# A streaming x + alpha·fx on one core: the first store on the ACT queue, beside an fx load, both in rows of 4096 bytes

## The chip, the cores and the metric

The kernel runs on one core of a Trainium2 chip. The metric is the device time of one execution in microseconds (us); lower is better. Each time is one execution; the time before is the median of three.

## What is computed

```
B, S, D = 512, 32, 640          # x, fx: bf16 [512, 32, 640]; alpha: bf16 [1]
def reference(x, fx, alpha):
    return x + alpha * fx
```

That is 10.5 million elements. Each of x, fx and the output is 20.97 MB, so 62.92 MB cross between HBM and the on-chip memory (SBUF), and each element gets one multiply and one add.

## The kernel before

The 16384 rows of 640 elements are spread over 128 partitions, so every partition owns one contiguous run of 81920 elements (163840 bytes) of x, of fx and of the output. The run is measured in columns of K = 1024 elements (2048 bytes), 80 in all. x is cut into three pieces, X = (0,32), (32,64), (64,80), and fx into five, FX = (0,16), (16,32), (32,51), (51,67), (67,80). Below, x0 to x2, f0 to f4 and s0 to s2 stand for the loads of these pieces and the stores of the three x pieces; `c j i` is the work of VectorE on the overlap of fx piece j and x piece i.

There are two buffers for x pieces and two for fx pieces. One instruction (`scalar_tensor_tensor`, line 92) computes fx·alpha + x and writes the sum over x in its buffer, and a store sends the whole x buffer to the output. alpha is spread over the partitions once by a 1x1 matmul at the start. So x2 goes into the buffer of x0 and may be loaded only after s0 has landed, f2 and f4 go into the buffer of f0 one after the other, and f3 goes into the buffer of f1, after `c 1 0` has read it.

The order of the work is written out by hand in `PLAN`; the tile framework adds the waits on data and buffers, but doesn't reorder. All transfers, loads and stores, are issued by the sync engine (SP), in the order of the plan:

```
x0  a  f0  f1  x1  [c 0 0]  f2  [c 1 0]  s0  f3  x2  [c 2 1]  f4  [c 3 1]  [c 3 2]  s1  [c 4 2]  s2
```

The steps in brackets are VectorE's. SP issues in order: when x2 waits for s0, all issues behind x2 (f4, s1, s2) wait too. The x0 load is cut in two, (0,4) and (4,32). Lines: 77 the x loads, 85 the fx loads, 92 the arithmetic, 104 the stores, 111 the load of alpha, 126 the closing wait of SP on all but the last store, 155 the end of the program.

A transfer goes as one descriptor for each partition, as long as its piece of the partition's run (up to 65536 bytes), and the 128 partitions are spread over 16 DMA engines: eight rows for each engine. The trace keeps one record for each descriptor, with its start, its duration and its size.

Of the kernel before, what the change touches and what calls it, by code (L numbers as in the profile page):

```python
# [2 lines left out]

# [4 lines left out]

ACT = mybir.ActivationFunctionType
ALU = mybir.AluOpType  # L10
F32 = mybir.dt.float32
BF16 = mybir.dt.bfloat16

K = 1024
P = 128


X = [(0, 32), (32, 64), (64, 80)]
FX = [(0, 16), (16, 32), (32, 51), (51, 67), (67, 80)]

X_CUTS = {0: (4,)}
PLAN = """
x 0
a
f 0
f 1
x 1
c 0 0
f 2
c 1 0  # L30
s 0
f 3
x 2
c 2 1
f 4
c 3 1
c 3 2
s 1
c 4 2
s 2  # L40
"""


@with_exitstack
def kernel(
    ctx: ExitStack,
    tc: tile.TileContext,
    x: bass.AP,
    fx: bass.AP,
    alpha: bass.AP,  # L50
    out: bass.AP,
):

    nc = tc.nc
    xv = x.flatten_outer_dims().rearrange("(p n) d -> p (n d)", p=P)
    fxv = fx.flatten_outer_dims().rearrange("(p n) d -> p (n d)", p=P)  # L60
    ov = out.flatten_outer_dims().rearrange("(p n) d -> p (n d)", p=P)
    assert xv.shape[1] == X[-1][1] * K == FX[-1][1] * K

    consts = ctx.enter_context(tc.tile_pool(name="consts", bufs=1))
    psum = ctx.enter_context(tc.tile_pool(name="psum", bufs=1, space=bass.MemoryType.PSUM))
    wide = ctx.enter_context(tc.tile_pool(name="wide", bufs=2))
    fs = ctx.enter_context(tc.tile_pool(name="fs", bufs=2))
    ctx.enter_context(tc.manual_schedule())

    xt, ft = {}, {}  # L70
    done = []

    def load_x(i):
        a, b = X[i]
        xt[i] = wide.tile([P, max(e - s for s, e in X) * K], x.dtype, tag="x", name="x_t")
        for c, d in pairwise((a, *X_CUTS.get(i, ()), b)):
            r = nc.sync.dma_start(  # L77
                out=xt[i][:, (c - a) * K : (d - a) * K], in_=xv[:, c * K : d * K]
            )
            done.append(r)  # L80

    def load_f(j):
        a, b = FX[j]
        ft[j] = fs.tile([P, max(e - s for s, e in FX) * K], fx.dtype, tag="f", name="f_t")
        r = nc.sync.dma_start(out=ft[j][:, : (b - a) * K], in_=fxv[:, a * K : b * K])
        done.append(r)

    def compute(j, i):
        (fa, fb), (xa, xb) = FX[j], X[i]
        a, b = max(fa, xa), min(fb, xb)  # L90
        piece = xt[i][:, (a - xa) * K : (b - xa) * K]
        r = nc.vector.scalar_tensor_tensor(  # L92
            out=piece,
            in0=ft[j][:, (a - fa) * K : (b - fa) * K],
            scalar=lanes["a_f"][:],
            in1=piece,
            op0=ALU.mult,
            op1=ALU.add,
        )
        done.append(r)  # L100

    def store(i):
        a, b = X[i]
        r = nc.sync.dma_start(out=ov[:, a * K : b * K], in_=xt[i][:, : (b - a) * K])
        done.append(r)

    lanes = {}

    def alpha_to_lanes():
        a_1 = consts.tile([1, 1], alpha.dtype, name="a_1")  # L110
        done.append(nc.sync.dma_start(out=a_1[:], in_=alpha[None, :]))  # L111
        ones = consts.tile([1, P], alpha.dtype, name="ones")
        nc.vector.memset(ones[:], 1.0)  # L113
        a_ps = psum.tile([P, 1], F32, name="a_ps")
        done.append(nc.tensor.matmul(a_ps[:], ones[:], a_1[:], start=True, stop=True))  # L115
        lanes["a_f"] = consts.tile([P, 1], F32, name="a_f")
        nc.vector.tensor_copy(out=lanes["a_f"][:], in_=a_ps[:])  # L117

    does = {"x": load_x, "f": load_f, "c": compute, "s": store, "a": alpha_to_lanes}
    for step in PLAN.split("\n"):  # L120
        if step:
            what, *of = step.split()
            does[what](*map(int, of))


    rest = nc.sync.nop(nofuse=True)
    info = mybir.DependencyInfo(mybir.DependencyClass.Sync, mybir.DependencyReason.DATA)
    for i in done[:-1]:
        tc.add_manual_dep(rest.ins, i.ins.name, info, reason="all but the last store")


# [1 line left out]
_INS = ['x', 'fx', 'alpha']  # L133
_OUTS = [((512, 32, 640), 'bfloat16')]


# [23 lines left out]
```

## Time and profile before

| | before |
|---|---|
| time, median of 3 (lowest to highest) | 151.99 us (151.99 to 152.27) |
| span of the profiled execution | 150.2 us |
| median less span | 1.8 us |
| VectorE busy | 86.8 us, 58% of the span |
| DMA bytes | 62.92 MB (41.94 MB read from HBM, 20.97 MB written) |
| share of 16 DMA engines' time in the span | 98.1% |
| mean rate | 419 GB/s |

The span runs from the first to the last instruction of the profiled execution. The profile has no other time for it; what lies around the span is taken as the median less the span, 1.8 us. VectorE, the only engine that does arithmetic on the data, is busy for little more than half of the span, while the DMA engines hardly rest.

### The profile page before, as it was taken

The numbers are of one execution on the slowest core, as the hardware profiler recorded it, in microseconds if no ns is written. First come the engines' busy times: TensorE is split into PE (matmuls) and PEld (weight loads), VectorE is DVE, ScalarE is ACT, GpSimd is POOL, SyncE is SP. The second block draws the span as 40 slices with busy tenths as digits, with TensorE's granted clock in tenths as the row PEclk, the third lists the DMA queues.
The fourth block names the chain that finished last, engine by engine and source line by source line (L and its number), as shares of the span: only waits on it lengthen the run. The fifth ranks groups of instructions, "written<-read, shape, count | busy, mean of one in ns | idle before, by whom it ended". The sixth has DMA issues, their size and how long they took to land.

```text
span 150.2 us, 78 instructions
## 1 busy us (share of the span) xinstructions
PE 0.2 (0%) x1; PEld 0.1 (0%) x1; DVE 86.8 (58%) x8; POOL 0.2 (0%) x4
## 2 busy tenths in 40 slices
PE   0000000000000000000000000000000000000000
PEld 0000000000000000000000000000000000000000
DVE  0000000049999999970399999106999999980000
POOL 0000000000000000000000000000000000000000
DMA  5997989999969696999696999999999969696994
GB/s 179 589 428 305 489 384 419 436 454 471 576 297 559 279 559 279 497 394 435 279 559 279 559 401 410 445 419 419 419 393 454 620 279 559 279 559 297 454 463 183
DMA packets 1730, 62.92 MB, mean 419 GB/s; under 512 B 194, under 2 KB 194, under 8 KB 194
## 3 DMA queue, kind: packets, MB, share of 16 engines
q1 hardware_dynamic: 1730, 62.92, 98.1%
HBM read 41.94 MB, written 20.97 MB: 419 GB/s over the span
## 4 chain that ended last, share of the span: by engine, by line
DMA 54%; DVE 35%; SPq 1%; issue 0%; DVEq 0%
DMA f_t<-in_fx_dram 54%; DVE x_t L92 35%; SPq L77 1%; SPq L111 0%; DVEq L92 0%
## 5 line engine op out<-in xcount | busy, mean ns | idle before, releaser
L92 DVE SCALAR_TENSOR_TENSOR x_t<-f_t,a_f,x_t 128x16384 bf16<-128x16384 bf16 (+3 forms) x6 | 86.5, 14438 | 25.5 <-DMA f_t<-in_fx_dram 25.5
L117 DVE COPY a_f<-a_ps 128x1 f32<-128x1 f32 x1 | 0.2, 159 | 21.5 <-PE a_ps L115 21.5
L113 DVE MEMSET ones<- 1x128 bf16 x1 | 0.2, 165 | 0.8 <-PEq L144 0.8
L115 PE MATMUL a_ps<-a,ones 1*128 1x1 bf16 x1 | 0.2, 158 | 22.2 <-DMA a<-in_alpha_dram 22.2
L144 POOL MEMSET const-bfloat16-1.0<- 128x1 bf16 x1 | 0.1, 103 | 0.0
L144 POOL MEMSET const-uint8-127<- 128x1 uint8 x1 | 0.1, 103 | 0.0
L115 PEld LDWEIGHTS <-ones 1*128 1x128 bf16 x1 | 0.1, 100 | 1.0 <-DVE ones L113 1.0
L144 POOL MEMSET const-float32-1.0<- 128x1 f32 x1 | 0.1, 100 | 0.0
L144 POOL MEMSET const-float32-0.0<- 128x1 f32 x1 | 0.1, 99 | 0.2 <-issue 0.2
## 6 DMA issues: line engine op xcount, KB each, us to landing
f_t<-in_fx_dram SPq DMA_DIRECT2D x3, 4096.0 KB, 35.6
x_t<-in_x_dram SPq DMA_DIRECT2D x1, 7168.0 KB, 21.3
f_t<-in_fx_dram SPq DMA_DIRECT2D x1, 4864.0 KB, 24.1
x_t<-in_x_dram SPq DMA_DIRECT2D x1, 4096.0 KB, 19.2
out_dram<-x_t SPq DMA_DIRECT2D x1, 4096.0 KB, 14.9
f_t<-in_fx_dram SPq DMA_DIRECT2D x1, 3328.0 KB
x_t<-in_x_dram SPq DMA_DIRECT2D x1, 1024.0 KB, 4.8
out_dram<-x_t SPq DMA_DIRECT2D x2, 24.7
```

The source lines that it names most:

```text
L77: r = nc.sync.dma_start(out=xt[i][:, (c - a) * K : (d - a) * K], in_=xv[:, c * K : d * K])
L92: r = nc.vector.scalar_tensor_tensor(out=piece, in0=ft[j][:, (a - fa) * K : (b - fa) * K], scalar=lanes["a_f"][:], in1=piece, op0=ALU.mult ...
L113: nc.vector.memset(ones[:], 1.0)
L115: done.append(nc.tensor.matmul(a_ps[:], ones[:], a_1[:], start=True, stop=True))
L117: nc.vector.tensor_copy(out=lanes["a_f"][:], in_=a_ps[:])
L144: nc = _bacc.Bacc("TRN2", target_bir_lowering=False, num_devices=1)
```

## The change

The store s0 is issued from the ACT engine's queue instead of SP's, and both s0 and the load f3 are described in rows of 4096 bytes: s0 goes from one descriptor of 65536 bytes for each partition to 16 of 4096, f3 from one of 32768 to 8 of 4096. All other transfers keep their queue and their rows. The plan keeps its order, and the waits on data and buffers stay what they were.

```diff
+RUN = 4096
+BESIDE = (3, 0)
 X_CUTS = {0: (4,)}
...
     def load_f(j):
         a, b = FX[j]
         ft[j] = fs.tile([P, max(e - s for s, e in FX) * K], fx.dtype, tag="f", name="f_t")
-        r = nc.sync.dma_start(out=ft[j][:, : (b - a) * K], in_=fxv[:, a * K : b * K])
+        run = RUN if j == BESIDE[0] else 65536
+        r = nc.sync.dma_start(
+            out=ft[j][:, : (b - a) * K], in_=fxv[:, a * K : b * K], max_dma_last_dim=run
+        )
         done.append(r)
...
     def store(i):
         a, b = X[i]
-        r = nc.sync.dma_start(out=ov[:, a * K : b * K], in_=xt[i][:, : (b - a) * K])
+        beside = i == BESIDE[1]
+        r = (nc.scalar if beside else nc.sync).dma_start(
+            out=ov[:, a * K : b * K],
+            in_=xt[i][:, : (b - a) * K],
+            max_dma_last_dim=RUN if beside else 65536,
+        )
         done.append(r)
```

## The prediction

> **What bounds the kernel now.** I read the page's DMA part first, because VectorE is busy for only 58% of the span.
>
> ```profile
> DMA  5997989999969696999696999999999969696994
> ...
> q1 hardware_dynamic: 1730, 62.92, 98.1%
> ...
> DMA 54%; DVE 35%; SPq 1%; issue 0%; DVEq 0%
> ```
>
> The second line is the one that matters: the packets of the only queue, SP's, occupy the 16 DMA engines for 98.1% of the span, 147.3 of 150.2 us. The third is the chain of waits, which passes through VectorE (DVE) for 35%; it takes VectorE as the last releaser wherever it can, but where the DMA engines work at the same time, VectorE's part is no slack to be won. To see whether they do, I asked for busy time in stretches that follow the transfers:
>
> ```profile
> core 0: us, PE busy (x) PEld busy (x) DVE busy (x) POOL busy (x), PEclk, DMA share, GB/s
> 0.00:2.00 2.00, 0.00 (x0) 0.10 (x1) 0.17 (x1) 0.20 (x4) 1.00 0.28 61
> 2.00:32.00 30.00, 0.16 (x1) 0.00 (x0) 0.16 (x1) 0.00 (x0) 1.00 1.01 433
> ...
> 69.00:74.00 5.00, 0.00 (x0) 0.00 (x0) 0.20 (x1) 0.00 (x0) 1.00 1.19 412
> 74.00:94.00 20.00, 0.00 (x0) 0.00 (x0) 20.00 (x1) 0.00 (x0) 1.00 0.97 419
> 94.00:104.00 10.00, 0.00 (x0) 0.00 (x0) 1.45 (x2) 0.00 (x0) 1.00 0.97 419
> ...
> 139.00:150.20 11.20, 0.00 (x0) 0.00 (x0) 0.00 (x0) 0.00 (x0) 1.00 0.83 357
> ```
>
> The column before the last is the DMA share (a packet counts where it starts, hence values above 1). After 2 us it is about 1 until the last store. From 94 to 104 VectorE does 1.45 us of work and the DMA share stays 0.97: VectorE waits for data, the DMA engines don't wait for anything. Then, for the order of things around the change, SP's own waits (us in total, times, longest) and the timeline (start, us):
>
> ```profile
> SPq L77 <- DMA out_dram<-x_t: 25.7, 1, 25.7
> ```
>
> ```profile
> 66.78 0.35 SPq L104 DMA_DIRECT2D out_dram<-x_t  x1
> 67.19 0.42 SPq L85 DMA_DIRECT2D f_t<-in_fx_dram  x1
> 73.80 20.48 DVE L92 SCALAR_TENSOR_TENSOR x_t<-f_t,a_f,x_t 128x19456 bf16<-128x19456 bf16 x1 [7.04 <-DMA f_t<-in_fx_dram]
> 93.37 0.33 SPq L77 DMA_DIRECT2D x_t<-in_x_dram  x1
> 102.84 17.41 DVE L92 SCALAR_TENSOR_TENSOR x_t<-f_t,a_f,x_t 128x13312 bf16<-128x13312 bf16 x2 [8.55 <-DMA f_t<-in_fx_dram]
> ```
>
> s0 and f3 are issued at 66.78 and 67.19, as `c 1 0` ends, and stand behind f2, which lands at 73.7. By the trace's packet records s0 then runs to 92.7, f3 to about 102.5, x2 to 112.1, f4 to 120.0, s1 to 139.3 and s2 to 149.0, each starting on every engine where the one before it stops. SP waits 25.7 us for s0 before it issues x2 (93.37), but f3 is queued behind s0 and runs for 9.7 us meanwhile, so this wait costs nothing now. VectorE's last piece ends at 134.5, 4.8 us before s1 has left the engines. So the end is set by bytes and packets alone: 62.92 MB at 433 GB/s is 145.3 us, and only idle DMA time or a change in the cost of a packet moves it.
>
> **The change part by part.** The sum is made on the profiled span of 150.2 us; 1.8 us around it bring it to the median of 151.99.
>
> *The issue moves to ACT.* One issue of 0.35 us leaves SP at 66.78 and appears on ACT, which has no other work in this kernel and waits for the same `c 1 0`. On SP nothing is left between f2 and f3, so f3 is issued some 0.4 us earlier; it still stands behind f2 in SP's ring. Both issues are covered by f2's transfer: 0. Without that cover it would be 0.35 us.
>
> *s0 starts beside f2.* In its own ring s0 needn't wait for f2. From issue to first packet the trace has one case on an idle ring, x0: issued at 0.73, first packet at 1.73, so 1.0 us. s0 starts at about 67.8, when each engine has two or three of f2's eight rows to begin. If the engines alternate by descriptors, s0 puts one of 4096 bytes between rows of 38912, and f2 lands 0.3 to 0.5 us later, at 74.2; `c 2 1` ends at 94.7 instead of 94.3. The work of the engines isn't more for it: 0 on the path.
>
> *f3 shares the engines with s0.* From about 73.7 both rings have rows of 4096 bytes. Alternating, f3's 64 per engine are through after 128 in all. VectorE's wait of 8.55 us before `c 3 1` goes: f3 lands at about 94.5, and `c 3 1` follows `c 2 1` at once, ends near 109 instead of 116.9, and s1 can be issued 8 us earlier. It stands in SP's ring behind x2 and f4, which are not through by then: 0. This is the visible gain of the change, and it is off the path.
>
> *More descriptors.* The packet records give 309 ns for 8192 bytes, 1213 for 32768 and 2418 for 65536, load or store alike. That is a line: (2418 - 309) / 57344 = 0.0368 ns per byte, and 309 - 301.3 = 7.7 ns for each descriptor. One of 4096 bytes then takes 150.6 + 7.7 = 158.3 ns. s0: 128 on each engine by 158.3 is 20.27 us, against 8 by 2418, 19.34: +0.92. f3: 64 by 158.3 is 10.13, against 8 by 1213, 9.70: +0.43. Together +1.35 us on engines that never rest. Bounds: 0, if the fixed part of one ring's row hides under the other's; 2.7, if every change of ring costs the 7.7 ns again. I take 1.35, the line through the rows.
> [...]
>
> *A new gap before x2.* x2 still waits for s0 to land, and SP holds f4, s1 and s2 behind it. Now f3 is no longer behind s0: it is finished when s0 still has about 60 rows per engine. s0 ends when the bytes of f2, s0 and f3 are through: at f3's old end of 102.5 plus 1.35, 103.85. Then both rings are empty. s0's last packet ended at 92.73 and its landing released SP at 93.35: 0.62 us. SP issues x2 0.02 us later (93.37), and the first packet follows 1.0 us after the issue, as for x0: 0.62 + 0.02 + 1.0 = 1.64 us in which no DMA engine works. Bounds: 0, if s0 ends before f3; 2.14, if x2 starts as slowly as x0, whose first rows averaged 371 ns instead of 309 (8 rows, 0.5 us). I take 1.64.
>
> *Loads and stores side by side.* The trace has no stretch with both directions for long. Bounds: a load and a store of the same row size take the same time (2418 for x1 and for s0), which reads like one stream in each engine, so 0 is nearest and I take it; above, rows as slow as x0's first (20% over) for the 20.3 us in which both rings are full would cost 4.1; below, see the rivals.
>
> *The sum.* 150.2 + 1.35 + 1.64 = 153.2 span, with 1.8 around it 155.0 us. Later steps move by the same 3.0 us: x2 from 105.5 to 115.2, f4 to 123.2, s1 to 142.4, s2 to 152.1. VectorE: `c 3 2` waits for x2 until 115.6, `c 4 2` for f4 until 123.5, ending at 137.6, still 4.8 us ahead of s1's end. One thing rides on top: f2's last two rows took about 1.7 and 2.5 us instead of 1.44 (the stretch 69 to 74 above), 1.3 us per engine that I can't explain. If that doesn't come back, all is 1.3 us earlier.
>
> **The rivals.**
>
> *No gap (0.12).* If an engine gives its rings turns by whole partition rows instead of descriptors, s0 (16 descriptors) gets twice f3's share, and its head start beside f2 makes it end first. x2 is then queued while f3 still runs, and only the descriptors cost: 151.99 + 1.35 = 153.3.
> [...]
>
> *Mixing is slow (0.14).* At 10% over, 20.3 us give 2.0 more: 157.0; at 20%, 159.1.
>
> *Mixing is fast (0.08), the other side.* A load writes SBUF and reads HBM, a store does the opposite; should the engines overlap them, the 20.3 us of shared work shrink. The 3.0 us of losses are paid back from 15% on; at a quarter, 5.1 us are saved and the time is 149.9. Against it: equal times in both directions, and no gap or overlap where store follows load in one ring.
>
> *No change (0.02).* A saving of about 15%, which just balances, or rows that the DMA merges again and no gap. Should the limit count elements instead of bytes, rows are 8192 bytes, the descriptors cost 0.62 and the time is 154.3, inside the forecast.
>
> **How the numbers follow.** The forecast, gap and descriptors with the shared stretch neutral, has 0.64 and its own range is 153.6 to 156.4: the low end is 155.0 less the 1.3 of f2's slow rows, the high end adds 1.35 for dearer changes of ring. The no-gap case at 153.3 goes in whole, and of slow mixing the smaller half, to 156.9. 153.0 to 156.9 leaves out fast mixing, no change and the worse half of slow mixing, less than 0.2. About 0.2% is what a measurement of this kernel can tell from no change. Slower by more: 0.64 + 0.12 + 0.14 = 0.90; within: 0.02; faster: 0.08.
>
> **What would show it.** Two DMA queues; packets up from 1730 by 2816 (3072 new, 256 gone), those under 8 KB from 194 to 3266. `c 3 1` starting within 0.1 us of the end of `c 2 1`, near 95. x2 issued near 104.5 instead of 93.4, with a dip of 1.6 us in the DMA share before its data, and no work in either ring. VectorE's waits moved to `c 3 2` (6 us) and `c 4 2` (4 us). Wrong would be: a DMA rate clearly over 433 GB/s from 74 to 95 (mixing is fast), one clearly under 410 (slow), or x2 issued while f3's data still come (no gap).

## The result and the profile after

The changed kernel takes 156.63 us (median of 4, 156.54 to 157.37) against 152.09 for the kernel before beside it: a ratio of 1.0306, 95% interval 1.0291 to 1.0322, or 4.5 us slower. The forecast was 155.0 in a range of 153.0 to 156.9. The profiled span went from 150.2 to 154.9.

The page's DMA part first. Queue q10 is ACT's; q1 is SP's.

```profile
DMA packets 4546, 62.92 MB, mean 406 GB/s; under 512 B 194, under 2 KB 194, under 8 KB 3266
...
q1 hardware_dynamic: 2482, 54.53, 83.9%
q10 hardware_dynamic: 2064, 8.39, 13.1%
```

There are 3072 new rows under 8 KB, and the two queues together fill 97.0% of a longer span: 150.3 us of packets instead of 147.3. So 3 us more of packet time and 1.7 us more of idle engines make up the difference. Stretches of the same form as before show where (the column before the last is the DMA share):

```profile
core 0: us, PE busy (x) PEld busy (x) DVE busy (x) POOL busy (x), PEclk, DMA share, GB/s
...
74.00:94.00 20.00, 0.00 (x0) 0.00 (x0) 19.86 (x1) 0.00 (x0) 1.00 1.02 422
94.00:104.00 10.00, 0.00 (x0) 0.00 (x0) 10.00 (x2) 0.00 (x0) 1.00 0.90 372
...
103.40:104.70 1.30, 0.00 (x0) 0.00 (x0) 1.30 (x1) 0.00 (x0) 1.00 0.00 0
```

From 74 to 94, where both rings are full, the rate is 422 GB/s: mixing loads and stores is neither fast nor slow here. (The same rows in one ring, in the run "rows alone" below, move 423 GB/s in this stretch.) VectorE is now busy from 74 on. From 103.4 to 104.7 no DMA engine does anything. The list of SP's waits and the timeline (start, us) show who waits for what:

```profile
SPq L79 <- DMA out_dram<-x_t: 36.5, 1, 36.5
```

```profile
94.54 14.08 DVE L97 SCALAR_TENSOR_TENSOR x_t<-f_t,a_f,x_t 128x13312 bf16<-128x13312 bf16 x1
103.78 0.34 SPq L79 DMA_DIRECT2D x_t<-in_x_dram  x1
104.22 0.37 SPq L88 DMA_DIRECT2D f_t<-in_fx_dram  x1
108.65 0.35 SPq L110 DMA_DIRECT2D out_dram<-x_t  x1
116.13 3.42 DVE L97 SCALAR_TENSOR_TENSOR x_t<-f_t,a_f,x_t 128x3072 bf16<-128x3072 bf16 x1 [7.51 <-DMA x_t<-in_x_dram]
125.16 14.09 DVE L97 SCALAR_TENSOR_TENSOR x_t<-f_t,a_f,x_t 128x13312 bf16<-128x13312 bf16 x1 [5.61 <-DMA f_t<-in_fx_dram]
```

`c 3 1` starts at 94.54, right behind `c 2 1`; the 8.55 us of waiting ahead of it are gone. They come back as 7.51 us ahead of `c 3 2` and 5.61 ahead of `c 4 2`. x2 is issued at 103.78 instead of 93.37, as s0 lands, with nothing else queued. s1 is issued at 108.65 instead of 116.95.

The packet records give the ends on the slowest engine:

| stage | ends before | ends after | what the stage adds |
|---|---|---|---|
| f2 | 73.4 | 73.5 | 0.1 |
| s0 and f3 | 102.4 | 103.4 | 0.85 |
| x2 | 112.1 | 115.7 | 2.65 |
| f4 | 120.0 | 124.8 | 1.23 |
| s1 | 139.3 | 144.2 | 0.0 |
| s2 | 149.0 | 153.8 | 0.0 |

The 2.65 of x2 are an empty stretch of 1.39 us (103.36 to 104.75) and 1.26 of late and slow first rows: they start between 104.75 and 105.79 and take up to 2.13 us instead of 1.21, on average over the engines 0.6 us too long. The 1.23 of f4 come from its last rows: 26624 bytes take 987 ns until 120.7, and then, after VectorE has gone idle and s1 has been queued for 12 us, 1.1 to 2.1 us.

### The profile page after: what moved, and what is told of

Same layout as the page of the kernel before. It is cut to its first block, busy times and chain, and to the rows that moved or that the text cites. A ratio compares the mean times of both kernels' runs of the same rounds, so it can differ in the third digit from the quotient of the medians.

```text
span 154.9 us, 80 instructions
## 1 busy us (share of the span) xinstructions
PE 0.2 (0%) x1; PEld 0.1 (0%) x1; DVE 86.8 (56%) x8; POOL 0.2 (0%) x4
## 4 chain that ended last, share of the span: by engine, by line
DMA 57%; DVE 31%; SPq 1%; issue 0%; DVEq 0%
DMA f_t<-in_fx_dram 33%; DVE x_t L97 31%; DMA out_dram<-x_t 24%; SPq L79 1%; SPq L121 0%; DVEq L97 0%; SPq L88 0%
```

## The experiments

Theories at this point. A: the order of the transfers costs. s0, now last to end, empties the rings ahead of x2, x2 then starts slowly, and an s1 that has been queued too long slows f4's last rows; the descriptors cost about 1 us. B: two rings of loads and stores cost by themselves. For the slow last rows there is also C: they go with an idle VectorE, or with the place of the rows.

**Rows alone.** The changed kernel with s0 back on SP:

```diff
-        r = (nc.scalar if beside else nc.sync).dma_start(
+        r = nc.sync.dma_start(
```

> The changed kernel with s0 back on the SP queue, rows of 4096 bytes for s0 and f3 kept. Theory: only the descriptors cost, 176 more per engine by 7.7 ns, +1.35 us in one ring, where nothing can hide the fixed part: 153.4 us; no gap before x2, f4's last rows at 987 ns. Rival: rows of this size cost nothing in one ring (152.1), or the gap comes from the rows (156).

Measured: 153.26 us, ratio 1.0078 (1.0063 to 1.0093), +1.2 us. s0 and f3 take 30.0 us on the slowest engine, from f2's end to their own, instead of 29.0; x2 starts without a gap at 103.1, f4's rows are at 991 ns on average. The rows in one ring cost about what the line through the packets said (1.35), somewhat less, and nothing else follows from them. The changed kernel differs from this run in nothing but the queue of s0, and takes 3.4 us more.

**Queue alone.** The changed kernel with the old rows:

```diff
-RUN = 4096
+RUN = 65536
```

> The changed kernel with the old rows (65536 bytes for s0, 32768 for f3), s0 still on the ACT queue. If the engines alternate between rings by descriptors, s0 gets two thirds of the shared time and ends about with f3, so x2 is issued when little or nothing of f3 is left: gap at most about 1.5 us plus slow first rows, no descriptor cost, f3 lands near 102, c 3 1 starts near 102.5, s1 is issued near 117 as before; 152 to 154 us. If they alternate by bytes, f3 ends near 93 as in the changed kernel, the gap stays, and the time is the changed kernel's 156.6 less the 0.8 of the descriptors: 155.8.

Measured: 154.84 us (154.24 to 155.12), ratio 1.0176 (1.0151 to 1.02), +2.8, above the 152 to 154 expected. The turns are by descriptor, as expected: s0's last row ends at 99.9, its landing releases SP at 101.4, and f3's last rows end between 101.9 and 102.4. x2's first rows start between 102.5 and 103.2, so an engine is empty for 0.5 us on average, though all of them together for only 0.1. x2's first rows are slow by some 0.7 us per engine on average, and f4's last rows by 1.1. The three make 2.3 us, as much as the profiled span grew (152.5 against 150.2). A load that found its engine empty started slowly here too, even where the other work ended only just ahead of it; and delaying x2 and f4 by 1 to 2 us while s1 is issued as before (116.78) was enough to bring f4's slow rows.

**f4 ahead of x2.** The plan of the changed kernel, reordered:

```diff
-x 2
 c 2 1
 f 4
+x 2
```

> The changed kernel with f4 issued ahead of x2 (plan: c 2 1, f 4, x 2). f4 waits for c 2 1 only, so SP issues it near 94.7 while s0 still runs, and x2 is queued behind it as s0 lands. Theory: the gap of 1.4 us and x2's slow first rows (together 2.65 us on the slowest engine) go: 154.0 us; the slow last rows of the load ahead of s1 (1.2 us) stay, now in x2. Rival: the gap is not what costs, and the time stays at 156.6.

Measured: 156.84 us, ratio 1.0308 (1.0293 to 1.0323): no gain, against 154.0 expected. The reason is in the packet records: while f4 (rows of 26624 bytes) runs beside s0 (4096), f4's rows start every 1.14 us, which is 0.987 + 0.159: one row of s0 for each of f4's. s0 gets 13% of the bytes and ends at 111.2 instead of 103.4, after f4 (107.3). x2 still waits for it:

```profile
94.65 0.34 SPq L88 DMA_DIRECT2D f_t<-in_fx_dram  x1
...
111.64 0.33 SPq L79 DMA_DIRECT2D x_t<-in_x_dram  x1
```

```profile
111.30:112.60 1.30, 0.00 (x0) 0.00 (x0) 0.00 (x0) 0.00 (x0) 1.00 0.00 0
```

The gap only moved, so this run says nothing about its price. As expected, the slow rows ahead of s1 moved to x2: s1 is issued at 112.06, and x2's last two rows take 1.8 and 2.0 us on average instead of 1.21. While both rings were full in this run, the one with rows of 4096 bytes got 13% of the bytes, the one with rows of 26624 the other 87%.

**x2 freed early.** s0 in two halves, and x2 in the first half of x0's buffer:

```diff
+S_CUTS = {0: (16,)}
...
+        if i == 2:
+            xt[i] = xt[0]
...
+        for c, d in pairwise((a, *S_CUTS.get(i, ()), b)):
             r = (nc.scalar if beside else nc.sync).dma_start(
...
```

> The changed kernel with s0 in two transfers on the ACT queue (columns 0 to 16 and 16 to 32, rows of 4096), and x2 loaded into the first half of x0's buffer, which is free when the first half has landed, near 94. The descriptor cost stays, the engines never run empty. Theory: the gap and x2's slow first rows (2.65 us on the slowest engine) go, the slow last rows of f4 ahead of the early s1 (1.2) stay: 154.1 us. Rival: without the gap nothing but the descriptors is left: 153.0; or two rings cost by themselves: 156.

Measured: 152.62 us, ratio 1.0045 (1.003 to 1.006): all but 0.7 us of the loss is gone, more than theory A said. The first half left earlier than I had reckoned with, after `c 0 0` at 49.8, and x2 was issued at 91.56:

```profile
91.56 0.34 SPq L83 DMA_DIRECT2D x_t<-in_x_dram  x1
96.15 0.33 SPq L92 DMA_DIRECT2D f_t<-in_fx_dram  x1
110.15 0.35 SPq L115 DMA_DIRECT2D out_dram<-x_t  x1
116.02 14.09 DVE L101 SCALAR_TENSOR_TENSOR x_t<-f_t,a_f,x_t 128x13312 bf16<-128x13312 bf16 x1 [2.57 <-DMA f_t<-in_fx_dram]
```

All rows of x2 and f4 take their usual 1213 and 987 ns. So two rings with small rows from 54 to 150 us cost no more than the descriptors, and theory B falls. f4's rows stayed fast though s1 was queued more than 5 us ahead of f4's end (115.5); what differs is that the second half of s0 ran beside them.

**s0 first.** The changed kernel with the old rows for s0, so that s0 gets nearly all of the bytes (65536 to f3's 4096, if the turns go by descriptor):

```diff
-            max_dma_last_dim=RUN if beside else 65536,
+            max_dma_last_dim=65536,
```

> The changed kernel with the old rows of 65536 bytes for s0 alone (still on the ACT queue; f3 keeps 4096). Turns by descriptor give s0 65536 bytes to f3's 4096, so s0 ends first, near 94, and x2 is queued behind f3, which ends near 103. Theory (gap, slow first rows of x2 and an s1 queued too early are what costs): none of the three is left, only f3's descriptors, +0.45: 152.5 us. Rival: two rings side by side cost by themselves, and the time stays over 154.

Measured: 152.59 us, ratio 1.0049 (1.0032 to 1.0065). s0 ends at 93.7, x2 is issued at 94.43 while f3 runs until 102.9, and x2 and f4 have their usual row times. Theory A's time held to 0.1 us; against the kernel before beside it, the run is 0.65 slower where 0.45 was expected.

```profile
94.43 0.34 SPq L79 DMA_DIRECT2D x_t<-in_x_dram  x1
```

```profile
94.00:104.00 10.00, 0.00 (x0) 0.00 (x0) 3.49 (x2) 0.00 (x0) 1.00 1.08 444
```

The DMA engines, which moved 372 GB/s from 94 to 104 in the changed kernel, now move 444. The two differ in s0's rows alone, and by them in which of two transfers ends first: 4 us. An estimated 0.8 of this is s0's share of the descriptors (120 of the 176 that cost 1.2 us in rows alone); the rest goes with the order.

**x2 freed early, old rows.**

```diff
-RUN = 4096
+RUN = 65536
```

> The kernel with s0 in two halves on the ACT queue and x2 in the first half's place, now with the old rows (32768 bytes for the halves of s0 and for f3). Theory: no gap, no slow first rows, and no added descriptors; what was left over of the time before in the 4096-byte form, some 0.7 us, goes: 151.9 us, or up to 1 us less if the slow last rows of f2 go as well. Rival: the rest was not the descriptors but the two rings, and the time stays at 152.6.

Measured: 156.64 us, ratio 1.0286 (1.026 to 1.0312): a miss, in a way that neither theory named. With rows of 32768 bytes the halves of s0 took every second turn and with it nearly half of the bytes (32768 to f2's 38912) from f2, which landed near 89.8 instead of 75.6, and VectorE became the bound:

```profile
89.83 51.80 DVE L101 SCALAR_TENSOR_TENSOR x_t<-f_t,a_f,x_t 128x19456 bf16<-128x19456 bf16 x4 [22.99 <-DMA f_t<-in_fx_dram]
```

```profile
121.60:125.10 3.50, 0.00 (x0) 0.00 (x0) 3.50 (x2) 0.00 (x0) 1.00 0.00 0
```

VectorE then works without a pause, s1 waits for it until 124.34, and the DMA engines are empty for 3.5 us. Rows of 4096 bytes do have their use here: a row of the store then takes 159 ns (s0, changed kernel) and not the 1213 of one of 32768 (s2, kernel before), and f2, beside it, landed 14.2 us earlier.

**s1 queued late.** The changed kernel with f4 in two parts, and s1 waiting for the first:

```diff
+F_CUTS = {4: (76,)}
+AFTER = {1: 4}
...
+        if i in AFTER:
+            tc.add_manual_dep(r.ins, parts[AFTER[i]][0].ins.name, info, reason="late")
```

> The changed kernel with f4 loaded in two parts, columns 67 to 76 and 76 to 80, and s1 made to wait for the first part, so that s1 reaches the ring some 1.5 us before f4's end and not 15 us before. Theory: a load's last two rows per engine are slow when a store has long been queued behind it; then f4's rows run at full rate and the time falls by 1.2 to 155.4. Rival: f4's rows are slow because VectorE idles or because of x2's late start; then the rows stay slow and the time stays at 156.6.

Measured: 155.53 us, ratio 1.0228 (1.0211 to 1.0245), 1.1 us less than the changed kernel, as theory A has it.

```profile
121.42 16.97 SPq L116 DMA_DIRECT2D out_dram<-x_t  x2
123.93 14.09 DVE L103 SCALAR_TENSOR_TENSOR x_t<-f_t,a_f,x_t 128x13312 bf16<-128x13312 bf16 x1 [4.57 <-DMA f_t<-in_fx_dram]
```

s1 is issued at 121.42, 2 us ahead of f4's end, and `c 4 2` starts at 123.93 instead of 125.16. All of f4's rows take their usual 686 and 309 ns, although VectorE is as idle as it was. Cutting f4 without the wait was not run in this kernel; for f2 in the kernel before, it was (below).

**The same cure in the kernel before.** f2's last two rows there were slow by 1.3 us, which the prediction couldn't explain. f2 is loaded in two parts and s0 waits for the first:

```diff
+F_CUTS = {2: (47,)}
+AFTER = {0: 2}
...
```

> The kernel before (all on SP, old rows) with f2 loaded in two parts, columns 32 to 47 and 47 to 51, and s0 made to wait for the first part: s0 reaches the ring about 1.5 us before f2's end instead of 6.6. Theory: a store that has long been queued slows the last two rows of the load ahead of it; f2's rows then all run at full rate (1.3 us per engine less), f2 lands near 72.4 and the time is 152.1 - 1.2 = 150.9. Rival: the slow rows come from elsewhere (VectorE's idle time, the addresses), and the time stays at 152.1 or rises by the 8 added descriptors, 0.06.

Measured: 151.08 us against 152.10, ratio 0.9938 (0.9925 to 0.995): 0.6% faster than the kernel before. f3, next in SP's order, was issued late together with s0 (70.61 instead of 67.19). Two controls: the cut without the wait,

```diff
-AFTER = {0: 2}
+AFTER = {}
```

> The kernel before with f2 loaded in the same two parts, and s0 issued as before at 66.8. Theory of the long queued store: the last rows ahead of s0 stay slow by about 1.2 us in total, 152.1 us. Rival: it is the long rows of f2 that are slow, and the cut alone mends it: 150.9.

and a copy on VectorE that fills its idle time while f2 arrives:

```diff
+COPY = 24 * K
...
 c 1 0
+b
...
+        piece = xt[1][:, :COPY]
+        done.append(nc.vector.tensor_copy(out=piece, in_=piece))
```

> The kernel before with one more VectorE copy (24 columns of x1's buffer onto themselves) right after c 1 0, so that VectorE works while f2's last rows arrive. Theory of the long queued store: f2's rows stay slow, 152.1. Rival, the slow rows come with an idle VectorE: f2's mean row falls from 1.60 to 1.44 us and the time to 150.9.

Both give 152.16, ratio 1.0004 (0.9995 to 1.0013). The start of `c 2 1` says when f2 has landed; first the late store, then the busy VectorE:

```profile
70.22 0.35 SPq L110 DMA_DIRECT2D out_dram<-x_t  x1
...
72.76 20.48 DVE L98 SCALAR_TENSOR_TENSOR x_t<-f_t,a_f,x_t 128x19456 bf16<-128x19456 bf16 x1 [6.19 <-DMA f_t<-in_fx_dram]
```

```profile
66.59 6.55 DVE L123 COPY x_t<-x_t 128x24576 bf16<-128x24576 bf16 x1
...
73.89 20.48 DVE L94 SCALAR_TENSOR_TENSOR x_t<-f_t,a_f,x_t 128x19456 bf16<-128x19456 bf16 x1 [0.74 <-DMA f_t<-in_fx_dram]
```

With s0 issued at 70.22 instead of 66.78, f2's rows are at full rate (30720 bytes in 1140 ns, 8192 in 313) and `c 2 1` starts at 72.76 instead of 73.80. With VectorE busy it starts at 73.89 and f2's rows average 1574 ns; with the cut alone, the eight short rows average 450 ns instead of 309. Theory C falls on both counts.

## Why the prediction was right, and where its sum was off

Direction and range held, but the range with some luck: 156.63 lies just above the forecast's own 153.6 to 156.4, and inside the whole range only because half of slow mixing, a rival that proved wrong, had been added to it. The course of events was the forecast's: f3 lands early, VectorE's wait ahead of `c 3 1` goes, and the gain is off the path, because s0 now ends last, alone, and x2 with all of SP's queue behind it waits for it. That this order is what costs is shown by the two runs that change it: s0 first (152.59) and x2 freed early (152.62).

- *More descriptors:* 1.35 taken, 0.85 measured on the slowest engine from f2's end on. Part of this is a head start: s0's first rows go out beside f2 from 70.8. In one ring the same rows cost 1.0 in the records and 1.2 in the time. The line was too high because it adds up durations that overlap: where the 4096-byte rows run in one ring (74.5 to 102 in rows alone), they come to 1.024 of the engines' time, against 1.002 for the long rows of before (4 to 66), some 0.7 us of 30.
- *The gap:* 1.64 taken, 1.39 measured. s0's landing followed its last packet after 0.35 us instead of the 0.62 assumed; the wake-up took 0.07 and the first packet 0.97 after the issue, where 1.0 was taken.
- *x2's slow start:* 0 taken, 0.5 kept as a bound; 0.6 on average over the engines, 1.26 on the slowest, and the slowest counts. The bound was an average where a maximum was wanted.
- *s1 issued 8 us earlier:* 0 taken, with the words that it "stands in SP's ring behind x2 and f4". This is the step that failed. Standing there wasn't free: it cost 1.1 us, as the late s1 shows. The trace of before had the same effect in front of s0, 1.3 us that I set aside as unexplained; it came back in the changed kernel, where f2's last rows lose 1.1 us per engine. A slow stretch that repeats at a handover deserved a bound wherever the change makes another handover of the kind.
- *Loads and stores side by side:* 0 taken, right: 422 GB/s, and 423 for the same rows in one ring.
- *s0 starts at 67.8:* it started at 70.8 on two engines, 4.0 us after its issue, and at 72.75 or later on the others, where the 1.0 us had been read off an idle ring. It cost nothing here.

The sum, 0.1 + 0.85 + 2.65 + 1.23 = 4.8 us, compares with 4.7 in the span and 4.5 in the medians; 3.0 were forecast. The rival of turns by whole partition rows is refuted by f4's 1.14 us in the run with f4 first. With the rows of these runs, 4096 bytes and more, it was one descriptor a turn: from 74 to 93 us in the changed kernel, 981 rows of s0 start and 978 of f3.

## What to carry to other kernels

This kernel keeps its DMA engines full (98.1% of the span before), and the earlier landing of f3 (`c 3 1` at 94.54 instead of 102.84) was worth nothing in it; look instead for which transfer ends last, and what the issuing queue holds back until then. Moving a transfer to a second queue changes that order: turns went by descriptor here, so the ring with the larger rows got more of the bytes (87% with f4 first), and a buffer's next load should wait for a transfer that ends while another is still running (152.59 us with s0 first, 156.63 with s0 last). Where a store has been queued for long behind a load, try issuing it some 2 us ahead of the load's end (151.08 instead of 152.10 us here).

## What the runs showed that I had not expected

A store queued long behind a load slowed the load's last rows: in the kernel before f2 by 1.3 us per engine, in the changed kernel f4 by 1.2 us, over the last 4 us or so of the load (78 and 53 KB per engine). Where the store was issued 2 to 3 us ahead of the load's end, there was next to none of it (f4 in the kernel before: issue at 116.95, end at 120.0). A load queued as long behind another load did no harm (f2 behind x1: issued at 49.59, x1's rows at 2419 ns). Nor does it take the same ring: in the changed kernel s0 stands in ACT's ring, and f2's rows ahead of its first packets lose 1.1 us all the same. In the run "x2 freed early, old rows" the loss fell on x1's rows, in the middle of that load, when the first half of s0 came in beside them: one row took 3.7 us on average instead of 2.4. The cause was not shown. A transfer that came in beside another ring's had its first packet 4.0 us after its issue (s0, changed kernel), 4.85 (s0, queue alone), 3.4 (f4, f4 first) and as much as 6.2 (s0, f4 first), against 1.0 on an idle ring (x0). It is open, too, why f4 was not slowed with x2 freed early, where s1 was queued more than 5 us ahead of f4's end with small rows of s0 beside it, while f2, with small rows of s0 beside it too, lost 0.8 us in the same run.
